# Half tiles of windowed attention: the globals' probabilities of four heads transposed as one 128x128 array instead of head by head

## The chip, the cores and the metric

The program runs on one core of a Trainium2 chip. The metric is the device time in microseconds of one execution. The kernel before has a median of 1014.69 us over 3 runs (1013.98 to 1016.17); one further execution was recorded by the profiler and took 1014.06 us.

## The reference

A windowed attention with global tokens feeds a two-layer network; the output is float32. There are 8 batches of 8 heads, 512 local tokens, 32 global tokens and 64 numbers per head. Local queries see the 32 globals and the local keys at most 32 positions away; global queries see everything.

```python
s_g  = scale * q_g @ concat(k_g, k_l).T          # 32 x 544 per head
s_l  = concat(scale * q_l @ k_g.T,               # 512 x 32: locals on globals
              where(|i - j| <= 32, scale * q_l @ k_l.T, -1e9))
out  = concat(softmax(s_g) @ v_all, softmax(s_l) @ v_all)   # v_all = concat(v_g, v_l)
x    = out as 4608 tokens x 512
h    = x @ w_in                                   # 512 x 2048
y    = elu(h) @ w_out                             # 2048 x 512
```

## The kernel before

Two streams of work share the engines. `attention()` (from L601) works in **tiles**: a tile is one batch, one group `g` of four heads, and 128 consecutive local queries `t` (0 to 3), so there are 8 x 2 x 4 = 64 tiles, 16 of them with t = 0. `ffn_stream()` (from L290) works through blocks of 256 tokens of the network: every float32 product there is three float16 matmuls of 256 columns (L306 for the first layer, L381 and L423 for the second). The program is written in turns of both streams (`pace`, L839), and a scheduler then fixes the order of each engine's queue, each served in order. While attention and network run, weights are loaded and converted to two float16 parts each (`unit`, L150 to L209), all of it early in the kernel.

A slot of attention is a tile or the global queries of a group (stage G, `stage_ga`, L625). The stages of a tile come in different slots:

- **S** (`stage_s`, L686): scores, 16 rows of L699; one array `p` holds, for each of the four heads, 128 columns of window keys and 32 columns of globals. VectorE masks and takes the maximum (L710), ScalarE exponentiates and sums (L717). Then `norm` (L720): VectorE forms 1/sum (L721, L722) and GpSimd scales the four heads' 160 columns (L724).
- **T** (`stage_t`, L730), two slots after S: four transposes of 128x128 turn the window part (L737); one copy puts them in `ptw` (L739).
- **U** (`stage_u`, L666), the same slot as T: the globals' part. For each head a matmul with the head's 32 columns as weights and the identity as the moving array puts 32 rows into PSUM (L673). In the tiles of t = 0 a 32x32 matmul for each head (L675) does the same with `pk`, the global queries' probabilities on the globals. One transpose (L676) turns `pg`, the global queries' probabilities on the tile's local keys. ScalarE copies to `ptw` (L677, L679) and `ptg` (L681; L684 for `pk`).
- **V** (`stage_v`, L742), one slot after T and U: 12 matmuls of `ptg` and `ptw` with the values (L766), and the copy to the network's input (L769).

A float32 matmul appears in the trace as two rows and a transpose as one, so U has 8 rows of L673, 8 of L675 where t = 0, and one of L676. The three `ptg` arrays are used alternately by the tiles of t > 0, the third by those of t = 0. In a loop of slots the stages are written in the order S, V, T, U (L823), loads two slots ahead (L799). All loads go through SyncE's queue; `qg`, the global queries, has two buffers (L616).

## Time and profile before

| | before |
|---|---|
| median of 3 runs | 1014.69 us |
| profiled execution | 1014.06 us |
| its span | 1012.3 us |
| TensorE busy | 979.0 us (97%) |
| VectorE busy | 737.2 us (73%) |
| ScalarE busy | 692.5 us (68%) |
| GpSimd busy | 248.1 us (25%) |

The span runs from the first to the last instruction; some 1.8 us of the execution's time lie around it. PE is TensorE's matmuls, PEld its weight loads (which run beside matmuls), DVE VectorE, ACT ScalarE, POOL GpSimd, SPq SyncE's DMA queue. Matmul rows are modelled to their end, so they overlap; what a step costs TensorE is read from start to start. In a row of the timeline, 128*32 is the part of the array in use (rows by columns), 128x128 the operand, x8 the number of merged rows.

### The profile page before, as it was taken

The page shows a single profiled execution, that of the slowest core. Times are in us where ns is not written, and L with a number is a line of the kernel's source. Part 1 is how long each engine was busy: PE and PEld are TensorE (multiplying, and loading weights), DVE is VectorE, ACT ScalarE, POOL GpSimd, SP SyncE. Part 2 cuts the span into 40 slices and gives each one's busy share as a digit, 9 for nine tenths or more (in the row PEclk, how much of TensorE's full clock was granted, in tenths as well). Part 3 has the DMA queues.
Part 4 walks back from the last instruction along what each step waited for, and adds up shares of the span by engine and source line. Part 5 has one row for each costly group of instructions (what it writes and reads, how often), then busy time and mean ns, then how long its engine had stood idle before and what let it go on. Part 6 is the DMA issues. An engine that isn't in the chain of part 4 may idle for free.

```text
span 1012.3 us, 24859 instructions
## 1 busy us (share of the span) xinstructions
PE 979.0 (97%) x9776; PEld 753.6 (74%) x9776; DVE 737.2 (73%) x2178; ACT 692.5 (68%) x1684; POOL 248.1 (25%) x435
## 2 busy tenths in 40 slices
PE   7799888999999999999999999999999999999997
PEld 3556555566666778877887888878878888888886
DVE  3757898999996667676776767676677758676665
ACT  4666968777666768676676667676776767677674
POOL 3534646626122111211212112111131121100000
PEclk9789998999999999999999999999999999999999
DMA  7645775653331123101420124112410111000000
GB/s 287 209 152 176 254 228 170 217 183 115 116 106 50 53 90 127 48 19 42 148 95 20 53 90 140 35 33 64 146 61 17 53 33 38 2 21 7 17 22 21
DMA packets 39372, 95.17 MB, mean 94 GB/s; under 512 B 5944, under 2 KB 6456, under 8 KB 39256
## 3 DMA queue, kind: packets, MB, share of 16 engines
q1 hardware_dynamic: 39064, 93.32, 27.2%
q8 instruction: 77, 1.26, 0.5%
q14 instruction: 39, 0.32, 0.1%
q10 hardware_dynamic: 144, 0.13, 0.0%
q0 software_dynamic: 48, 0.13, 0.0%
HBM read 78.36 MB, written 15.20 MB: 92 GB/s over the span
## 4 chain that ended last, share of the span: by engine, by line
PE 77%; DVE 8%; ACT 5%; issue 5%; POOL 2%; DMA 1%; POOLq 0%; ACTq 0%; DVEq 0%
PE h L306 27%; PE acc L423 12%; PE pa L766 6%; PE h L423 6%; PE acc L381 5%; PE pa L673 4%; PE pa L699 4%; PE pa L423 3%; PE pa L737 3%; PE pa L306 2%; PE pa L634 2%; PE pa L676 1%; POOL p L724 1%; PE h L766 1%; PE pa L675 1%
## 5 line engine op out<-in xcount | busy, mean ns | idle before, releaser
L306 PE MATMUL h<-xh,winh 128*128 128x256 f16 x992 | 271.5, 274 | 5.9 <-ACT hs L316 5.7
L306 PE MATMUL h<-xh,winl 128*128 128x256 f16 x992 | 270.7, 273 | 0.8 <-DVE winl L200 0.8
L306 PE MATMUL h<-xl,winh 128*128 128x256 f16 x992 | 270.8, 273 | 0.4 <-DVE xl L512 0.4
L306 PEld LDWEIGHTS <-winh 128*128 128x128 f16 x2176 | 209.5, 99 | 46.7 <-issue 15.5
L724 POOL TENSOR_SCALAR p<-p,sm 128x160 f32<-128x160 f32 x256 | 130.8, 528 | 433.9 <-DVE sm L722 198.2
L324 DVE SCALAR_TENSOR_TENSOR g<-g,hs 128x512 f32<-128x512 f32 x136 | 94.1, 692 | 125.8 <-ACT g L317 125.5
L423 PEld LDWEIGHTS <-gh 128*128 128x128 f16 x1456 | 140.4, 99 | 23.6 <-issue 6.1
L717 ACT ACTIVATE p<-p,m 128x160 f32<-128x160 f32 x256 | 106.4, 418 | 69.5 <-DVE m L713 68.9
L315 ACT ACTIVATE g<-h,xs 128x512 f32<-128x512 f32 x124 | 84.8, 684 | 53.0 <-PE h L306 51.9
L306 PEld LDWEIGHTS <-winl 128*128 128x128 f16 x1088 | 106.8, 98 | 15.5 <-DVE winl L200 1.4
L327 DVE SCALAR_TENSOR_TENSOR gl<-gs,xs,gh 128x640 f16<-128x640 f32 x104 | 93.0, 894 | 30.2 <-ACT gh L346 29.9
L346 ACT ACTIVATE gh<-gs,xs 128x640 f16<-128x640 f32 x104 | 86.3, 829 | 32.3 <-DVE gs L342 32.3
L345 ACT ACTIVATE gh<-g,xs 128x256 f16<-128x256 f32 x104 | 53.2, 512 | 56.0 <-DVE g L324 55.7
L423 PE MATMUL acc<-wouth,gh 128*128 128x256 f16 (+1 forms) x312 | 88.0, 282 | 0.2 <-ACT gh L346 0.2
L317 ACT ACTIVATE g<-g 128x512 f32<-128x512 f32 x136 | 85.5, 629 | 0.0
L423 PE MATMUL acc<-wouth,gl 128*128 128x256 f16 x312 | 85.0, 273 | 0.2 <-DVE gl L327 0.2
L316 ACT ACTIVATE hs<-h,xs 128x512 f32<-128x512 f32 x124 | 84.4, 681 | 1.0 <-POOL xs L526 1.0
L423 PE MATMUL acc<-woutl,gh 128*128 128x256 f16 x312 | 85.0, 273 | 0.0
L423 PEld LDWEIGHTS <-gl 128*128 128x128 f16 x728 | 71.2, 98 | 12.9 <-DVE gl L327 0.5
L327 DVE SCALAR_TENSOR_TENSOR gl<-g,xs,gh 128x256 f16<-128x256 f32 (+1 forms) x136 | 75.8, 558 | 6.9 <-ACT gh L331 3.4
L710 DVE CUSTOM_DVE_ANT_0 p<-pa,msk 128x160 f32<-128x160 f32 x228 | 62.2, 319 | 13.1 <-PE pa L699 13.0
L766 PE MATMUL pa<-ptw,v 128*64 128x96 f32 x864 | 54.0, 246 | 0.0
(217 smaller groups left out, 2037.1 us busy)
## 6 DMA issues: line engine op xcount, KB each, us to landing
v<-vT SPq DMA_DIRECT2D x64, 384.0 KB, 3.2
k<-kT SPq DMA_DIRECT2D x32, 640.0 KB, 5.1
q<-qT SPq DMA_DIRECT2D x32, 256.0 KB, 5.3
raw<-w_in SPq DMA_DIRECT2D x8, 1024.0 KB, 6.5
raw<-w_out SPq DMA_DIRECT2D x8, 1024.0 KB, 5.3
out<-o SPq DMA_DIRECT2D x32, 256.0 KB, 2.3
od<-o SPq DMA_DIRECT2D x24, 256.0 KB, 4.0
o<-od SPq DMA_DIRECT2D x24, 256.0 KB, 3.2
```

The source lines that it names most:

```text
L306: nc.tensor.matmul(h[:, j, :], wt[:, c, f], xt[:, c, :], start=k == 0, stop=k == 11)
L315: nc.scalar.activation(g, hf, AF.Relu, scale=sc[:, p:p + 1])
L316: nc.scalar.activation(hs, hf, AF.Copy, scale=sc[:, 2 * NP + 1 + p:2 * NP + 2 + p])
L317: nc.scalar.activation(g, g, AF.Exp, scale=-1.0)
L324: nc.vector.scalar_tensor_tensor(out=g, in0=g, scalar=-1.0, in1=hs, op0=ALU.add, op1=ALU.max)
L327: nc.vector.scalar_tensor_tensor(out=dst, in0=src, scalar=sg, in1=hi, op0=ALU.mult, op1=ALU.subtract)
L346: nc.scalar.activation(gh[:, 2:7, :], s, AF.Copy, scale=sg)
L423: nc.tensor.matmul(cols, gt, w, start=first, stop=last and k == len(todo) - 1)
L710: nc.vector.tensor_tensor_reduce(out=p, in0=sp[r][:, j * KW:(j + 1) * KW], in1=msk[:, mi, :], op0=ALU.add, op1=ALU.max, scale=1.0, scalar= ...
L717: nc.scalar.activation(ps[i], ps[i], AF.Exp, bias=m[:, 1, i:i + 1], scale=scale, accum_out=s[:, 0, i:i + 1])
L724: nc.gpsimd.tensor_scalar(ps[i], ps[i], s[:, 1, i:i + 1], 1.0, ALU.mult, ALU.mult)
L766: nc.tensor.matmul(pv[64 * r:64 * r + 64, o], w, x, start=i == 0, stop=i == 2)
```

## The change

The globals' part of `p` gets an array of its own, `pz` (128 queries x 4 heads x 32 globals), which VectorE writes normalized in one operation with 1/sum as a broadcast operand. GpSimd then scales only the 128 window columns. U turns `pz` with one transpose of 128x128. The exponentials of the global queries on the globals go into `pu`, and four GpSimd operations write them, normalized, into the diagonal blocks of a 128x128 array `pk` whose other entries are zero; U turns that with one transpose, and VectorE adds up its four column blocks into `ptg`. To make room in memory, there are two `ptg` instead of three (one for the tiles of t > 0, one for t = 0), and `qg` has one buffer.

```diff
-    ptg = [wts.tile([P, PW], F32, name=f"ptg{i}") for i in range(3)]
+    ptg = [wts.tile([P, PW], F32, name=f"ptg{i}") for i in range(2)]
...
+    pkd = [wts.tile([P, P], F32, name=f"pk{i}") for i in range(2)]
+    for p in (*ptg, *pkd):
         nc.gpsimd.memset(p, 0.0)
...
-            qg = apool.tile([P, 2, SG], F32, name="qg", bufs=2)
+            qg = apool.tile([P, 2, SG], F32, name="qg", bufs=1)
...
-            pk = apool.tile([P, 32], F32, name="pk")
+            pk = pkd[g]
+            pu = apool.tile([P, 32], F32, name="pu", bufs=1)
...
-                nc.gpsimd.tensor_scalar(pk, pk, s[:, 3:4], 1.0, ALU.mult, ALU.mult)
+                for h in range(4):
+                    q = slice(32 * h, 32 * h + 32)
+                    nc.gpsimd.tensor_scalar(pk[q, q], pu[q, :], s[q, 3:4], 1.0, ALU.mult, ALU.mult)
...
-            for h in range(4):
-                q = slice(32 * h, 32 * h + 32)
-                nc.tensor.matmul(tp[q, P:2 * P], st["p", g, t][:, h, P:KW], ident, start=True, stop=True)
-                if t == 0:
-                    nc.tensor.matmul(tp[q, 2 * P:2 * P + 32], pk[q, :], ident[q, q], start=True, stop=True)
+            nc.tensor.transpose(tp[:, P:2 * P], st["pz", g, t].rearrange("p h x -> p (h x)"), ident)
+            if t == 0:
+                nc.tensor.transpose(tp[:, 2 * P:3 * P], pk, ident)
...
-                nc.scalar.copy(pz[:, HQ:HQ + 32], tp[:, 2 * P:2 * P + 32])
+                nc.vector.tensor_reduce(out=pz[:, HQ:HQ + 32], in_=tp[:, 2 * P:3 * P].rearrange("p (h q) -> p q h", h=4),
+                                        op=ALU.add, axis=AX.X)
...
-                    nc.gpsimd.tensor_scalar(ps[i], ps[i], s[:, 1, i:i + 1], 1.0, ALU.mult, ALU.mult)
+                    nc.gpsimd.tensor_scalar(ps[i][:, 0:P], ps[i][:, 0:P], s[:, 1, i:i + 1], 1.0, ALU.mult, ALU.mult)
+                pz = st["pz", g, t] = apool.tile([P, 4, 32], F32, name="pz")
+                nc.vector.tensor_tensor(out=pz, in0=pp[:, :, P:KW], in1=s[:, 1, :].unsqueeze(2).to_broadcast([P, 4, 32]),
+                                        op=ALU.mult)
...
-            pt, pz = st["pt", g, t] = ptw[n % 2], ptg[2 if t == 0 else n % 2]
+            pt, pz = st["pt", g, t] = ptw[n % 2], ptg[t == 0]
```

Line numbers from the changed kernel are a few higher than those of before: L673 and L675 there become L675 (`pz`) and L677 (`pk`), L676 becomes L678, L737 L743, L766 L772, L699 L702, L423 L424.

Where both streams run densely, the queue of TensorE read like this before, at the U of a tile with t > 0 (`gh` and `gl` are the first layer's outputs in two parts, loaded as the array's weights; `raw` here holds sums of the second layer's weights, `h` a bank of PSUM):

```order
L423 LDWEIGHTS gl
L423 MATMUL h<-raw,gl 128x256
L673 MATMUL pa<-ident,p 32x128 x4
L676 MATMUL pa<-ident,pg 128x128
L423 LDWEIGHTS gh
L423 MATMUL pa<-raw,gh 128x256
```

and now, at the same tile:

```order
L424 LDWEIGHTS gl
L424 MATMUL h<-raw,gl 128x256
L675 MATMUL pa<-ident,pz 128x128
L678 MATMUL pa<-ident,pg 128x128
L424 LDWEIGHTS gh
L424 MATMUL pa<-raw,gh 128x256
```

Four matmuls became one transpose, and the neighbours stand where they stood. From the U of the 21st tile on (44 of the 64), TensorE's queue differs in the U stages alone.

At the start of the kernel TensorE's queue had this, the end of the U of the first tile, T and U of the second, and then the first V (`h<-ptg`, `h<-ptw`; the rows of L699 are the S of later tiles):

```order
L676 MATMUL pa<-ident,pg 128x128
L737 MATMUL pa<-ident,p 128x128 x4
L673 MATMUL pa<-ident,p 32x128 x4
L676 MATMUL pa<-ident,pg 128x128
L699 MATMUL acc<-k,q 64x160 x4
L699 MATMUL pa<-k,q 64x160
L699 MATMUL acc<-k,q 64x160 x4
L766 MATMUL h<-ptg_85,v 64x160 x2
L766 MATMUL h<-ptw_81,v 64x96 x4
```

and now has, from the U of the first tile:

```order
L675 MATMUL pa<-ident,pz 128x128
L677 MATMUL pa<-ident,pk_89 128x128
L678 MATMUL pa<-ident,pg 128x128
L743 MATMUL pa<-ident,p 128x128 x4
L772 MATMUL h<-ptg_84,v 64x160 x2
L772 MATMUL h<-ptw_81,v 64x96 x4
L772 MATMUL h<-ptg_84,v 64x160 x2
L772 MATMUL h<-ptw_81,v 64x96 x4
L702 MATMUL acc<-k,q 64x160 x4
L675 MATMUL pa<-ident,pz 128x128
L678 MATMUL pa<-ident,pg 128x128
```

The first V moved ahead of the second tile's U, and the order of the first 20 tiles, among the weights' conversion, was drawn up anew in such places.

On VectorE, in the dense part, the new operation stands right behind 1/sum (`sm`) and ahead of the low float16 parts `gl`, which the second layer's matmuls take:

```order
L343 TENSOR_TENSOR gs<-g 128x128
L724 TENSOR_SCALAR sm<-sm 128x4
L725 RECIPROCAL sm<-sm 128x4
L729 TENSOR_TENSOR pz<-p,sm 128x128
L328 SCALAR_TENSOR_TENSOR gl<-g,xs,gh 128x256
L328 SCALAR_TENSOR_TENSOR gl<-gs,xs,gh 128x640
```

There the rows of before read the same without L729.

More of the change, by code (lines that the diff above doesn't have):

```diff
@@ L108, in attn_ffn @@
         nc.gpsimd.memset(p[0:HQ, 1, :], 0.0)
-    for p in ptg:
+    pkd = [wts.tile([P, P], F32, name=f"pk{i}") for i in range(2)]
+    for p in (*ptg, *pkd):
         nc.gpsimd.memset(p, 0.0)
@@ L652, in ex @@
                                          AF.Exp, bias=m[:, 3:4], scale=scale, accum_out=s[:, i:i + 1])
-                nc.scalar.activation(pk, halves[0][:, NT * HQ:NT * HQ + 32], AF.Exp, bias=m[:, 3:4], scale=scale,
+                nc.scalar.activation(pu, halves[0][:, NT * HQ:NT * HQ + 32], AF.Exp, bias=m[:, 3:4], scale=scale,
                                      accum_out=s[:, 2:3])
```

## Prediction

> **What bounds the kernel now.** First the busy times in four stretches, then the chain of waits in the same stretches. Columns of the windows: length, then busy time and instructions of PE, PEld, DVE, ACT and POOL, then the granted TensorE clock, DMA share and GB/s.
>
> ```profile
> 0.00:95.00 95.00, 81.07 (x845) 50.28 (x846) 56.95 (x260) 54.91 (x201) 37.82 (x85) 0.86 0.58 202
> 95.00:235.00 140.00, 128.44 (x1084) 82.67 (x1083) 128.46 (x333) 109.31 (x237) 79.87 (x100) 0.98 0.65 217
> 235.00:870.00 635.00, 633.60 (x6611) 500.55 (x6609) 458.19 (x1379) 437.50 (x1099) 124.41 (x241) 1.00 0.20 68
> 870.00:1012.00 142.00, 135.86 (x1244) 120.06 (x1241) 93.62 (x211) 90.78 (x150) 5.95 (x10) 0.99 0.05 16
> ```
>
> From 235 us to 870 us TensorE is busy for 633.6 of 635 us, while VectorE and ScalarE have a quarter to a third of their time free. What leaves TensorE there leaves the kernel. Between 95 and 235 us the weights are converted: TensorE and VectorE are each busy for 128 of 140 us, and neither alone sets the end. In the head, up to 95 us, TensorE works for 81 us at a clock of 0.86. After 870 us no attention is left. The chain of waits says the same for the head and the dense stretch, in this order (shares of the stretch by line):
>
> ```profile
> by line: PE h L766 12.3%; PE pa L673 10.9%; PE pa L737 8.7%; PE pa L634 7.4%; PE pa L699 6.9%; PE h L306 5.4%; PE acc L133 4.7%; POOL p L724 4.1%; PE acc L699 3.5%; PE pa L676 3.5%; PE pa L675 3.3%; DVE p L710 2.9%; DVE cu L179 2.6%; issue
> ...
> by line: PE h L306 36.7%; PE acc L423 14.7%; PE pa L766 9.2%; PE h L423 7.3%; PE acc L381 6.7%; PE pa L699 4.3%; PE pa L673 4.0%; PE pa L423 3.6%; PE pa L737 2.9%; PE pa L676 1.8%; PE pa L634 1.4%; PE pa L675 1.1%; ACT hs L316 0.7%; ACT p L
> ```
>
> In the head the three lines of stage U (L673, L675, L676) make 17.7% of the chain, 16.8 us of 95: U is on the path there too.
>
> How many tiles lie where comes from the rows of L673 and L675 in the four stretches (PE busy and rows, PEld busy and rows):
>
> ```profile
> 0.00:95.00 95.00, 12.57 (x96) 4.07 (x96) 0.86 0.58 202
> 95.00:235.00 140.00, 5.80 (x64) 2.04 (x64) 0.98 0.65 217
> 235.00:870.00 635.00, 30.72 (x352) 10.84 (x352) 1.00 0.20 68
> ...
> 0.00:95.00 95.00, 4.30 (x32) 2.38 (x32) 0.86 0.58 202
> 95.00:235.00 140.00, 1.95 (x16) 1.06 (x16) 0.98 0.65 217
> 235.00:870.00 635.00, 9.74 (x80) 5.29 (x80) 1.00 0.20 68
> ```
>
> A tile has eight rows of L673, and with t = 0 also eight of L675. That makes 12 tiles in the head (4 with t = 0), 8 in the middle (2), and 44 in the dense stretch (10).
>
> **What a U costs, and what it will cost.** The timeline of TensorE shows a U of t > 0, a U of t = 0 and, for comparison, a stage T of four full transposes:
>
> ```profile
> 408.89 0.27 PE L423 MATMUL acc<-cu,gl 128*128 128x256 f16 x1
> 409.09 0.43 PE L673 MATMUL pa<-ident,p 128*32 128x128 f32 x8
> 409.45 0.33 PE L676 MATMUL pa<-ident,pg 128*128 128x128 f32 x1
> 409.62 0.27 PE L423 MATMUL h<-wouth,gh 128*128 128x256 f16 x1
> ...
> 326.51 0.27 PE L306 MATMUL h<-xh,winl 128*128 128x256 f16 x1
> 326.71 0.41 PE L673 MATMUL pa<-ident,p 128*32 128x128 f32 x2
> 327.05 0.24 PE L675 MATMUL pa<-ident,pk 32*32 32x32 f32 x2
> ...
> 328.75 0.33 PE L676 MATMUL pa<-ident,pg 128*128 128x128 f32 x1
> 328.92 0.27 PE L306 MATMUL h<-xh,winh 128*128 128x256 f16 x1
> ...
> 405.83 0.27 PE L306 MATMUL h<-xh,winl 128*128 128x256 f16 x1
> 405.94 0.60 PE L737 MATMUL pa<-ident,p 128*128 128x128 f32 x4
> 406.38 0.27 PE L306 MATMUL h<-xh,winh 128*128 128x256 f16 x1
> ```
>
> A float16 matmul occupies TensorE for 0.11 us (405.83 to 405.94). So the U of t > 0 takes from 408.89 + 0.11 = 409.00 to 409.62, 0.62 us, and the U of t = 0 from 326.62 to 328.92, 2.30 us: there the pieces alternate between 32 columns of all rows and 32x32 corners, and each pair takes 0.5 us. The four transposes of T take 0.44 us, 0.11 each, with no gap on either side. After the change U consists of such transposes alone, two or (t = 0) three: 0.22 or 0.33 us. The saving is 0.40 us for t > 0 and 1.97 us for t = 0. The other bound is L676's own 0.17 us for each transpose (409.45 to 409.62), behind narrow matmuls: 0.28 and 1.79 us. I take T's, since the new transposes stand among full-array work.
>
> - **Dense stretch:** 10 x 1.97 + 34 x 0.40 = 33.3 us (by the other bound 10 x 1.79 + 34 x 0.28 = 27.4). TensorE's order there changes in nothing else. I take 33.
> - **Head:** 4 x 1.97 + 8 x 0.40 = 11.1 us at full clock, 12.9 at 0.86. From it go the three debits below; I take 7.
> - **Middle:** 2 x 1.97 + 6 x 0.40 = 6.3 us of TensorE work, but other engines end last there, and VectorE gets 8 `pz` and 2 reductions more; I take 2, with bounds of 6 either way because the order is drawn anew.
>
> **The other terms.** The nearest rows for the new VectorE operations, and for what GpSimd and ScalarE change (in the rows with three numbers, durations are ns minimum/median/maximum):
>
> ```profile
> L342 DVE TENSOR_TENSOR gs<-g x104: 270/284/703, 333.1 to 1001.9; 128x128 f32<-128x128 f32 x104
> L121 DVE TENSOR_REDUCE xm<-pa 128x1 f32<-128x128 f32 x16 | 4.5, 282 | 3.3 <-PE pa L120 3.1
> L684 ACT COPY ptg<-pa 128x32 f32<-128x32 f32 x16 | 3.1, 192 | 0.0
> L724 POOL TENSOR_SCALAR p<-p,sm x256: 387/398/1879, 13.9 to 846.5; 128x160 f32<-128x160 f32 x128
> L660 POOL TENSOR_SCALAR pk<-pk,sg x16: 285/656/970, 12.6 to 776.3; 128x32 f32<-128x32 f32 x16
> PEld pa L737 <- POOL p L724: 10.5, 15, 4.3
> ```
>
> VectorE gains 64 x 0.28 us + 16 x 0.28 = 22 us (64 `pz` at up to 0.70 make 45), ScalarE loses 16 x 0.19 = 3 us. In the dense stretch 44 + 10 of these are 15 us on an engine with 177 us free; there `gl` comes 0.28 us later, which the weights loaded two steps behind cover. Without that cover it would cost 44 x 0.28 = 12 us. In the middle the cover is thin: 10 x 0.28 = 2.8 us, already inside my 2.
>
> GpSimd scales 128 instead of 160 columns, which is below 0.40 us an operation, and writes `pk` in four pieces instead of one: 3 x 0.29 = 0.9 us more per group at best, 3 x 0.97 = 2.9 at worst, ahead of `pg` and of `p` in its queue. With GpSimd at a fifth of the dense stretch this is hidden. In the head T waits for `p` (10.5 us over the whole head and 15 times, in the last row), and four groups there cost between nothing and 4 x 2.9 = 12 us; I take 1, since a group's `pk` and `pg` are usually done before the next `sm` comes.
>
> `pz` is written in the same moment as GpSimd scales the same tile. L724's spread, 398 at the median and 1879 at the most, and L342's 703 beside its 284 say that both can stretch when they meet. I charge the head 2 us (12 tiles of some 0.2), bounded by 0 and 12 x 0.42 = 5. On this the Trainium skill (GPSIMD Engine Reference, Specifications) says that GpSimd's memory interfaces are shared with VectorE, with contention for VectorE instructions that read two arrays from SBUF, as the new one does and the old GpSimd-only way did not. The rows above agree in that durations spread.
>
> The single `qg` buffer makes the second `qg` load wait for the first G to end, with the keys of the second group and the first weights behind it in SyncE's queue:
>
> ```profile
> 4.75 0.49 SPq L617 DMA_DIRECT2D qg<-qgT  x1
> 7.44 0.39 PE L634 MATMUL pa<-k,qg 64*32 64x256 f32 x2
> 12.86 0.41 PE L634 MATMUL pa<-k,qg 64*32 64x256 f32 x2 [3.35 <-ACT p L717]
> k<-kT SPq DMA_DIRECT2D x32, 640.0 KB, 5.1
> ```
>
> The load moves from 4.75 to 7.44 + 0.39 = 7.8 us, 3.1 us later. The two key loads behind it then land near 7.8 + 0.5 + 1.9 (their two issues) + 5.1 = 15.3 us; the second G starts at 12.86 now. So the cost lies between 0 and 3 us; I take 2. Debits of the head: 1 + 2 + 2, and 1 for idle time that stays: 12.9 - 6 = 7.
>
> One `ptg` for all tiles of t > 0: ScalarE's copy of U (L681) must now wait for V of the tile before, and behind it in ScalarE's queue stand the network's exponentials. V comes first in TensorE's queue anyway; it costs nothing as long as that gap stays (the last rival).
>
> **Sum:** 33 + 7 + 2 = 42 us; 1014 - 42 = **972 us** against the profiled execution's 1014.06, which lies 0.6 us under the median. A difference of 0.2%, 2 us, is about what a measurement of this kernel tells from none.
>
> **The rivals.**
>
> 1. *Only the dense stretch gains (chance 0.18).* The head's savings are taken by `p` and the keys arriving later, and the new order of the middle gives back up to 6. For it: 14 us of the head without TensorE work, and VectorE as full as TensorE in the middle. Against it: U's 17.7% of the head's chain. Time: 1014 - 33 = 981, up to 1014 - 33 + 6 = 987.
> 2. *Everything counts (0.08).* The head's 12.9 and the middle's 6 come in full: 1014 - 33 - 13 - 6 = 962. For it: TensorE is busy for 128 of 140 us in the middle. Against it: the debits.
> 3. *The clock falls (0.03).* Transposes replace matmuls in the head, and if these did not keep the clock up, the head's 81 busy us at 0.86 would run at the 0.7 of the second slice: 81 x 0.86 / 0.7 = 99.5, 18 us longer. Time: 1014 - 33 - 2 + 18 = 997, still faster.
>
> ```profile
> PEclk9789998999999999999999999999999999999999
> ```
>
>    Against it: T, L676 and every other transpose run now at a granted clock of 1.00. The rule behind it is the Trainium skill's (TensorE: Matmul & The Clock Gate, Part 4: PE-mode transpose): transposes do not count as busy for the clock. In the dense stretch a U's 0.2 us is too short to show it, so the row for 235 to 870 us neither proves nor excludes it.
> 4. *The single `ptg` stalls ScalarE (0.02), the one that ends slower.* Place: L681 behind V.
>
> ```profile
> 403.86 0.50 PE L766 MATMUL pa<-ptw,v 128*64 128x96 f32 x8
> ```
>
>    V of the tile before ends at 404.36, U starts at 409.09: 4.7 us to spare. If V came behind U's copy instead, ScalarE would hold the network's work for each tile. To turn 42 us into a loss TensorE would have to stand still for 42 / 64 = 0.66 us a tile; at 1 us a tile the time is 1014 - 42 + 64 = 1036.
>
> That TensorE's work would not get shorter at all is no case of its own: the U rows and T's rows lie a factor of two to seven apart, and L676's 0.17 us is the worst that a transpose costs.
>
> **Chances.** The forecast has 0.67, with a range of its own from 964 to 980 (the bounds of the head's debits, 7 with 1 to 13, and of the middle in part). Half of rival 1 up to 986 and most of rival 2 belong to the range: 961 to 986. Rivals 1 to 3 and the forecast all end faster; slower has rival 4's 0.02 and 0.01 for what is not foreseen, and 0.01 stays for no change, which makes 0.96, 0.01 and 0.03.
>
> **What would show it.** In the profile after: U of t > 0 from start to start 0.22 us and U of t = 0 0.33 us, with no gap ahead; the dense stretch (from the 21st tile's U on) shorter by 33 us, with TensorE still at 99%; L729 near 0.28 us and VectorE's busy time up by some 22 us; the second G starting 2 us later. Wrong would be: waits of PE for ACT or DVE in the dense stretch of over 5 us, transposes at 0.17 us, a lower clock in the head, or a middle that is longer than 140 us.

## The result, and the profile after

The changed kernel takes 973.72 us (median of 4 runs, 973.07 to 977.49) against 1015.43 us for the kernel before (4 runs, 1013.98 to 1016.25): a ratio of 0.9598, with an interval of 0.9571 to 0.9626. Its profiled execution took 974.17 us, with a span of 972.1 us; before it was 1014.06 and 1012.3. Forecast were 972 us, in a range of 961 to 986. Three executions on record stand far off all others (1112.72 and 3332.99 us of the kernel before, 1116.83 us of the one with one `qg` buffer); the ratios leave them out, and without them the medians given here change by less than 0.1 us.

First the four stretches in the windows of the changed kernel, cut at the places in its work that are nearest to those shown of before (columns as there):

```profile
0.00:89.00 89.00, 69.31 (x781) 46.92 (x781) 64.71 (x288) 59.11 (x207) 47.35 (x103) 0.90 0.67 233
89.00:225.00 136.00, 119.21 (x975) 78.00 (x974) 124.35 (x331) 104.79 (x225) 72.70 (x103) 0.97 0.64 216
225.00:830.00 605.00, 601.84 (x6224) 492.89 (x6223) 467.44 (x1431) 434.02 (x1088) 135.85 (x270) 1.00 0.21 71
830.00:972.00 142.00, 135.69 (x1242) 119.89 (x1240) 93.81 (x211) 90.90 (x150) 5.96 (x10) 0.99 0.05 16
```

TensorE is still busy for 99% of the dense stretch, which is 30 us shorter. The clock did not fall: 0.90 in the head, where it was 0.86, 0.97 in the middle, where it was 0.98, and 1.00 in the dense stretch. GpSimd now works for 47 us in a head of 89 us. The stretch without attention is as long as before.

The timeline of TensorE shows a U of t > 0 and a U of t = 0:

```profile
402.55 0.27 PE L307 MATMUL h<-xh,winl 128*128 128x256 f16 x1
402.66 0.27 PE L675 MATMUL pa<-ident,pz 128*128 128x128 f32 x1
402.77 0.27 PE L678 MATMUL pa<-ident,pg 128*128 128x128 f32 x1
402.88 0.27 PE L307 MATMUL h<-xh,winh 128*128 128x256 f16 x1
...
423.11 0.27 PE L307 MATMUL h<-xh,winl 128*128 128x256 f16 x1
423.22 0.27 PE L675 MATMUL pa<-ident,pz 128*128 128x128 f32 x1
423.33 0.27 PE L677 MATMUL pa<-ident,pk 128*128 128x128 f32 x1
423.44 0.27 PE L678 MATMUL pa<-ident,pg 128*128 128x128 f32 x1
423.55 0.27 PE L424 MATMUL acc<-wouth,gh 128*128 128x256 f16 x1
```

From start to start that is 0.22 and 0.33 us, 0.11 for each transpose, without a gap on either side. U took 0.62 and 2.30 us before.

For an account by place the same U is looked up in both traces. These are the U of the 21st and of the 64th tile, in the kernel before:

```profile
269.96 0.43 PE L673 MATMUL pa<-ident,p 128*32 128x128 f32 x8
...
868.90 0.42 PE L673 MATMUL pa<-ident,p 128*32 128x128 f32 x8
```

and in the changed kernel:

```profile
259.94 0.27 PE L675 MATMUL pa<-ident,pz 128*128 128x128 f32 x1
...
829.03 0.27 PE L675 MATMUL pa<-ident,pz 128*128 128x128 f32 x1
```

The 21st U comes 10.0 us earlier. From there to the 64th it was 598.94 us and is 569.09, 29.85 us less. Behind the 64th the last 143.4 us became 143.1, one U's worth. That makes 40.2 us, the difference of the spans.

The new and changed operations, each grouped over the whole span (ns minimum/median/maximum):

```profile
L729 DVE TENSOR_TENSOR pz<-p,sm x64: 274/291/419, 13.6 to 810.1; 128x128 f32<-128x128 f32 x64
L686 DVE TENSOR_REDUCE ptg<-pa x16: 276/282/292, 19.8 to 777.5; 128x32 f32<-128x128 f32 x16
L664 POOL TENSOR_SCALAR pk<-pu,sg x64: 282/294/2257, 12.5 to 743.9; 32x32 f32<-32x32 f32 x64
L727 POOL TENSOR_SCALAR p<-p,sm x256: 368/375/2046, 14.8 to 808.1; 128x128 f32<-128x128 f32 x128
```

VectorE's operations cost what the nearest rows had said, 0.29 and 0.28 us. GpSimd's pieces of `pk` are 0.29 us at the median, but up to 2.26. VectorE's busy time rose from 737.2 to 750.3 us, by 13 us and not by the 22 of the forecast, though the two new groups make 64 x 0.291 + 16 x 0.282 = 23 us; neighbouring rows overlap in the trace, and how much of the difference that explains stays open.

The second `qg` load in the timeline of SyncE's queue, and the second G in that of TensorE:

```profile
8.02 0.33 SPq L618 DMA_DIRECT2D qg<-qgT  x1
```

```profile
14.60 1.07 PE L635 MATMUL pa<-k,qg 64*32 64x256 f32 x4 [5.19 <-DMA k<-kT]
```

The load moved from 4.75 to 8.02 us, and the second G from 12.86 to 14.60.

TensorE's waits in the dense stretch, before (the stretch from 235 to 870 us) and after (225 to 830 us); the numbers are us in total, times, the longest:

```profile
PE h L306 <- ACT hs L316: 1.1, 3, 0.5
```

```profile
PE h L307 <- ACT hs L317: 2.8, 6, 0.9
```

It is one wait in both kernels: the first layer's matmuls need a bank of PSUM that ScalarE still reads for `hs`. It became longer. In the chain of waits ScalarE and VectorE now have a larger place in this stretch, where the first of them was `hs` with 0.7% before (shares by line):

```profile
by line: PE h L307 27.5%; PE acc L424 11.2%; PE pa L772 7.2%; PE h L424 5.6%; DVE gl L328 3.7%; PE acc L382 3.5%; ACT p L720 3.3%; PE pa L702 3.2%; DVE g L325 2.8%; PE pa L424 2.7%; DVE p L713 2.4%; issue 2.2%; PE pa L743 2.2%; DVE cu L260 
```

The longest of these waits, from the timeline of the changed kernel (start, duration, engine; in brackets the idle time ahead and what ended it):

```profile
761.50 0.32 DVE L713 CUSTOM_DVE_ANT_0 p<-pa,msk 128x160 f32<-128x160 f32 x1
762.54 0.16 DVE L716 TENSOR_SCALAR m<-m 128x4 f32<-128x4 f32 x1
762.79 0.43 ACT L720 ACTIVATE p<-p,m 128x160 f32<-128x160 f32 x1 [1.48 <-DVE m L716]
...
764.71 0.68 ACT L316 ACTIVATE g<-h,xs 128x512 f32<-128x512 f32 x1
...
764.84 0.27 PE L424 MATMUL pa<-raw,gl 128*128 128x256 f16 x1
...
765.29 0.68 ACT L317 ACTIVATE hs<-h,xs 128x512 f32<-128x512 f32 x1
...
766.01 0.27 PE L307 MATMUL h<-xh,winh 128*128 128x256 f16 x1 [0.90 <-ACT hs L317]
```

Read upwards: TensorE stands from 764.95 to 766.01 us for `hs`; `hs` stands in ScalarE's queue behind four exponentials of S (L720); and the first of those waited 1.48 us for the maxima, which VectorE had in its own queue. Counted from start to start, matmuls that came more than 0.35 us after the one ahead were 4 between the 21st and the 64th U before, and 8 after, all of them of the first layer. Beyond a matmul's 0.11 us they cost 1.9 us before and 4.4 us after. Below these are called the stalls.

### The profile page after: what moved, and what is told of

It reads as the page before. It is cut to its first block, busy times and chain, and to the rows that moved or that the text cites. A ratio compares the mean times of both kernels' runs of the same rounds, so it can differ in the third digit from the quotient of the medians.

```text
span 972.1 us, 23882 instructions
## 1 busy us (share of the span) xinstructions
PE 926.0 (95%) x9216; PEld 737.7 (76%) x9216; DVE 750.3 (77%) x2258; ACT 688.8 (71%) x1668; POOL 261.9 (27%) x484
## 4 chain that ended last, share of the span: by engine, by line
PE 60%; DVE 18%; ACT 10%; issue 7%; DMA 4%; POOL 1%; SPq 0%; POOLq 0%; DVEq 0%; ACTq 0%
PE h L307 21%; PE acc L424 10%; PE pa L772 5%; PE h L424 5%; PE acc L382 4%; PE pa L702 3%; ACT p L720 3%; DVE gl L328 3%; PE pa L307 2%; PE pa L424 2%; PE pa L743 2%; DVE g L325 2%; DVE p L713 2%; PE pa L635 2%; DVE cu L260 1%
## 5 line engine op out<-in xcount | busy, mean ns | idle before, releaser
L307 PEld LDWEIGHTS <-winh 128*128 128x128 f16 x2176 | 208.8, 98 | 47.0 <-issue 16.1
L727 POOL TENSOR_SCALAR p<-p,sm 128x128 f32<-128x128 f32 x256 | 124.7, 505 | 374.7 <-DVE sm L725 142.3
L424 PEld LDWEIGHTS <-gh 128*128 128x128 f16 x1456 | 139.2, 98 | 23.6 <-issue 6.1
L720 ACT ACTIVATE p<-p,m 128x160 f32<-128x160 f32 x256 | 106.3, 418 | 60.6 <-DVE m L716 59.8
L307 PEld LDWEIGHTS <-winl 128*128 128x128 f16 x1088 | 106.8, 98 | 14.4 <-DVE winl L201 1.0
L424 PE MATMUL acc<-wouth,gh 128*128 128x256 f16 (+1 forms) x312 | 88.0, 282 | 0.2 <-ACT gh L347 0.2
L424 PE MATMUL acc<-wouth,gl 128*128 128x256 f16 x312 | 85.1, 273 | 0.2 <-DVE gl L328 0.2
L424 PE MATMUL acc<-woutl,gh 128*128 128x256 f16 x312 | 85.0, 273 | 0.0
L424 PEld LDWEIGHTS <-gl 128*128 128x128 f16 x728 | 71.2, 98 | 12.9 <-DVE gl L328 0.5
L664 POOL TENSOR_SCALAR pk<-pu,sg 32x32 f32<-32x32 f32 x64 | 41.0, 640 | 66.4 <-ACT gh L347 24.5
```

The source lines that it names most:

```text
L307: nc.tensor.matmul(h[:, j, :], wt[:, c, f], xt[:, c, :], start=k == 0, stop=k == 11)
L424: nc.tensor.matmul(cols, gt, w, start=first, stop=last and k == len(todo) - 1)
L720: nc.scalar.activation(ps[i], ps[i], AF.Exp, bias=m[:, 1, i:i + 1], scale=scale, accum_out=s[:, 0, i:i + 1])
L727: nc.gpsimd.tensor_scalar(ps[i][:, 0:P], ps[i][:, 0:P], s[:, 1, i:i + 1], 1.0, ALU.mult, ALU.mult)
```

## The experiments

The first question was why U had been so dear. The theory, at which the prediction only hints ("the pieces alternate"): the change of the array's shape between 128x32 and 32x32 costs the time, not the number of rows. The rivals: the sixteen small matmuls themselves cost it, so that only leaving them out helps; or the gain comes from what VectorE takes off GpSimd. The second question was where the dense stretch lost 3 us, and what the head really paid. Numbers of all runs stand in a table at the end of this section.

**The kernel before, with the matmuls of U sorted by shape.** No work is removed.

```diff
             for h in range(4):
                 q = slice(32 * h, 32 * h + 32)
                 nc.tensor.matmul(tp[q, P:2 * P], st["p", g, t][:, h, P:KW], ident, start=True, stop=True)
-                if t == 0:
-                    nc.tensor.matmul(tp[q, 2 * P:2 * P + 32], pk[q, :], ident[q, q], start=True, stop=True)
+            for h in range(4 if t == 0 else 0):
+                q = slice(32 * h, 32 * h + 32)
+                nc.tensor.matmul(tp[q, 2 * P:2 * P + 32], pk[q, :], ident[q, q], start=True, stop=True)
```

> The kernel before, with one edit: in the U of t = 0 the four 32x32 matmuls of pk stand behind the four matmuls of p instead of between them. No work is removed. Theory 1 (a U of t = 0 took 2.30 us because TensorE changes eight times between 32 columns of all rows and 32x32 corners, at some 0.2 us a change, and the matmuls themselves are cheap): the U of t = 0 falls to about 0.9 us, 1.4 us x 16 = 22 us less TensorE work, of which 14 lie in the dense stretch and most of the other 8 in the head; time 995 to 998. Theory 2 (each of the 16 rows costs its 0.1 us wherever it stands): the U stays above 2 us, time within 3 us of before.

Measured: 992.24 us, ratio 0.9779 (0.9756 to 0.9802). The U of t = 0 in its timeline of TensorE:

```profile
318.41 0.43 PE L673 MATMUL pa<-ident,p 128*32 128x128 f32 x8
318.76 0.26 PE L676 MATMUL pa<-ident,pk 32*32 32x32 f32 x8
318.96 0.33 PE L677 MATMUL pa<-ident,pg 128*128 128x128 f32 x1
319.12 0.27 PE L306 MATMUL h<-xh,winh 128*128 128x256 f16 x1
```

The same seventeen rows take 0.71 us (318.41 to 319.12) instead of 2.2, and the dense stretch is 14.4 us shorter (584.55 us). That the rows cost their time wherever they stand is refuted: sorting alone gives 22.7 of the change's 41 us by the medians. The total came out 3 us below the range that was expected. On this the Trainium skill (TensorEngine Tiling (Array Packing), Key Properties) says that changing the tiling mode drains the TensorE; the trace agrees in that seven changes between the two shapes became one, and 1.5 us went, 0.25 for each of the six. The rows also show what a change spoils. One 128x32 matmul by itself lasts 0.41 us (the row at 326.71 of the kernel before, x2), and four side by side last 0.43 (409.09, x8); with 32x32 it is 0.24 (327.05, x2) and 0.26 (318.76, x8). Four of a shape that stand together run nearly as one, and a matmul of the other shape between them prevents it. How much of the 0.25 us is the change itself and how much this lost overlap, no run here separates.

**The change without the block-diagonal array**: `pz` with one transpose, `pk` as before but its four matmuls together.

```diff
-            pk = pkd[g]
+            pk = apool.tile([P, 32], F32, name="pk")
...
-                for h in range(4):
-                    q = slice(32 * h, 32 * h + 32)
-                    nc.gpsimd.tensor_scalar(pk[q, q], pu[q, :], s[q, 3:4], 1.0, ALU.mult, ALU.mult)
+                nc.gpsimd.tensor_scalar(pk, pk, s[:, 3:4], 1.0, ALU.mult, ALU.mult)
...
-                nc.tensor.transpose(tp[:, 2 * P:3 * P], pk, ident)
+                for h in range(4):
+                    q = slice(32 * h, 32 * h + 32)
+                    nc.tensor.matmul(tp[q, 2 * P:2 * P + 32], pk[q, :], ident[q, q], start=True, stop=True)
...
-                nc.vector.tensor_reduce(out=pz[:, HQ:HQ + 32], in_=tp[:, 2 * P:3 * P].rearrange("p (h q) -> p q h", h=4),
-                                        op=ALU.add, axis=AX.X)
+                nc.scalar.copy(pz[:, HQ:HQ + 32], tp[:, 2 * P:2 * P + 32])
...
```

> The changed kernel without the block-diagonal pk: pk is normalized and transposed as before, by four 32x32 matmuls, but these now stand together behind the transpose of pz. Theory 1 (changes of the array's mode are what costs): the U of t > 0 takes 0.22 us and that of t = 0 about 0.7 us, so TensorE saves 48 x 0.40 + 16 x 1.6 = 45 of the 50.6 us; time about 978. Theory 2 (the pk matmuls themselves cost): the U of t = 0 stays near 1.9 us, the saving is 48 x 0.40 + 16 x 0.4 = 26 us, time about 992.

Measured: 972.51 us, 0.9594 (0.957 to 0.9618), not to be told from the whole change, and 5 us below the expected 978. Its U of t = 0:

```profile
309.65 0.27 PE L671 MATMUL pa<-ident,pz 128*128 128x128 f32 x1
309.85 0.26 PE L675 MATMUL pa<-ident,pk 32*32 32x32 f32 x8
310.04 0.33 PE L676 MATMUL pa<-ident,pg 128*128 128x128 f32 x1
310.21 0.27 PE L306 MATMUL h<-xh,winh 128*128 128x256 f16 x1
```

0.56 us against the change's 0.33: over the dense stretch's ten that is 2.3 us, of which 0.8 come back as shorter stalls (570.58 against 569.09 us in all). Before the 21st U this kernel is 5.6 us ahead, but its profiled execution had a clock of 0.97 up to there, against 0.95, which makes some 5 us. So the block-diagonal array, its four pieces on GpSimd and its sum on VectorE bring nothing over a sorted order that these runs can show.

**The change without `pz`**: the globals by four matmuls, GpSimd scaling all 160 columns, `pk` block-diagonal.

```diff
-            nc.tensor.transpose(tp[:, P:2 * P], st["pz", g, t].rearrange("p h x -> p (h x)"), ident)
+            for h in range(4):
+                q = slice(32 * h, 32 * h + 32)
+                nc.tensor.matmul(tp[q, P:2 * P], st["p", g, t][:, h, P:KW], ident, start=True, stop=True)
...
```

> The changed kernel without pz: GpSimd scales all 160 columns again, and U turns p by four matmuls of 32 columns, then pk by one transpose of 128x128. By the sum over start-to-start times: U of t > 0 stays at 0.62 us, that of t = 0 falls from 2.30 to about 0.73 us, 16 x 1.57 = 25 us of TensorE work; 16 of it in the dense stretch, so 994 to 998. If instead the gain of the change came from VectorE's pz (an earlier, cheaper GpSimd scaling) and not from TensorE's rows, this kernel would stay within 5 us of before.

Measured: 989.31 us, 0.9758 (0.9733 to 0.9783). U takes 0.62 us for t > 0 as before, and 0.72 with `pk`'s transpose; 583.42 us lie between the 21st and the 64th U. More than half of the gain is there although VectorE and GpSimd work on `p` as they did before. That this gain comes from what VectorE takes off GpSimd is refuted. The dense stretch is 15.5 us shorter, as expected (16); the total lies 5 us below the expected range, and what is more lies ahead of the 21st U, where this execution's clock was 0.97 instead of 0.94.

**The change with two `qg` buffers** (and two `m` and `sm` instead of three, to make room).

```diff
-            qg = apool.tile([P, 2, SG], F32, name="qg", bufs=1)
+            qg = apool.tile([P, 2, SG], F32, name="qg", bufs=2)
...
-            m = apool.tile([P, 2, 4], F32, name="m", bufs=3)
-            s = apool.tile([P, 2, 4], F32, name="sm", bufs=3)
+            m = apool.tile([P, 2, 4], F32, name="m", bufs=2)
+            s = apool.tile([P, 2, 4], F32, name="sm", bufs=2)
```

> The changed kernel with two buffers for qg again (the space comes from two instead of three buffers for m and sm). Theory 1 (the second qg load waits for the first G, and the keys of the second group with it): the second qg load is issued near 4.8 instead of 8.0 us, the second G starts near 12.9 instead of 14.6 us, and the head is 1.5 to 2 us shorter: 971.5 to 972.5. Theory 2 (GpSimd's scaling decides when the first T's start, whatever the second G does): the second G starts earlier and the time stays within 0.7 us of the changed kernel's 973.7.

Measured: 974.30 us, 0.9603 (0.9578 to 0.9628). The second G starts at 12.61 us instead of 14.60, and the time stays. The late load is real and costs nothing that these runs can show. The buffers also changed the order of TensorE's queue at some places between 36 and 52 us, so this is not the load alone.

**ScalarE relieved**: U's copy of the globals on VectorE in the dense part (there `tab` holds an "f").

```diff
-            nc.scalar.copy(pz.rearrange("p (a x) -> p a x", a=2)[:, :, 0:HQ],
-                           tp[:, P:2 * P].rearrange("p (a q) -> p a q", a=2))
+            copy = nc.vector.tensor_copy if "f" in tab else nc.scalar.copy
+            copy(pz.rearrange("p (a x) -> p a x", a=2)[:, :, 0:HQ],
+                 tp[:, P:2 * P].rearrange("p (a q) -> p a q", a=2))
```

> The changed kernel with U's copy to ptg moved from ScalarE to VectorE where both streams run densely (44 or so copies of 0.27 us); TensorE's order is the same. It asks why the dense stretch became 30 us shorter and not 33: in the changed kernel TensorE waits there 2.8 us, six times, for hs of the network's first layer (ScalarE). Theory 1 (ScalarE is late because VectorE is: before hs, ScalarE's queue stands idle for the scores' maxima m): VectorE gets fuller, the six waits stay or grow, from the U of tile 21 to that of tile 64 it takes 569 us or more; time 973.5 to 977. Theory 2 (ScalarE has too much work): the waits fall below 1 us, this stretch takes 566.5 us, time 971.

Measured: 977.98 us, 0.9651 (0.9618 to 0.9684). The waits of TensorE between 270 and 840 us:

```profile
PE h L307 <- ACT hs L317: 2.7, 7, 0.6
PE pa L773 <- DVE ptg L684: 2.0, 2, 1.1
```

The wait for `hs` stays, and V now waits for `ptg` on VectorE. Of this kernel's 14 stalls 8 are of the first layer, 4.1 us, as many as in the change (4.4 us). It isn't the amount of ScalarE's work that stalls TensorE.

**`pz` written twice**, the same operation two times in a row.

```diff
                 nc.vector.tensor_tensor(out=pz, in0=pp[:, :, P:KW], in1=s[:, 1, :].unsqueeze(2).to_broadcast([P, 4, 32]),
                                         op=ALU.mult)
+                nc.vector.tensor_tensor(out=pz, in0=pp[:, :, P:KW], in1=s[:, 1, :].unsqueeze(2).to_broadcast([P, 4, 32]),
+                                        op=ALU.mult)
```

> The changed kernel with the VectorE operation that writes pz done twice for each tile (64 x 0.28 = 18 us more on VectorE, 12 of them between the U of tile 21 and that of tile 64); the output is the same. Theory 1 (VectorE's added work is hidden up to the waits for hs, which come from VectorE): the dense stretch goes from 569 to 570 to 573 us, the part before it gets up to 3 us longer, time 974 to 979. Theory 2 (wholly hidden): 973.7 within 1 us. Theory 3 (VectorE is on the path everywhere): 12 us in the dense stretch alone, time 986 or more.

Measured: 978.53 us, 0.9638 (0.9598 to 0.9677). Between the 21st and the 64th U lie 568.82 us, as without the second copy; the 4.8 us by the medians can only lie outside that stretch. That was a miss: an effect in the dense stretch had been expected too. The 4.8 us are no price of the operation: the ratio's interval overlaps the change's (0.9571 to 0.9626), the runs go from 973.92 to 981.25 us, and TensorE's order was drawn anew from 39 us on.

**`pz` by GpSimd in the dense part**, four operations a tile.

```diff
+                if "f" in tab:
+                    for i in range(4):
+                        nc.gpsimd.tensor_scalar(pz[:, i, :], pp[:, i, P:KW], s[:, 1, i:i + 1], 1.0, ALU.mult, ALU.mult)
+                else:
+                    nc.vector.tensor_tensor(out=pz, in0=pp[:, :, P:KW],
+                                            in1=s[:, 1, :].unsqueeze(2).to_broadcast([P, 4, 32]), op=ALU.mult)
```

> The changed kernel with pz written by GpSimd (four operations of 32 columns) instead of VectorE where both streams run densely; TensorE's order there is the same. Theory 1 (the 3 us missing in the dense stretch are VectorE's added 0.28 us a tile): the waits for hs fall to the 1.1 us of before, from the U of tile 21 to that of tile 64 it takes 567 us instead of 569, time 971.5 to 972.5. Theory 2 (they come from TensorE reaching the network's matmuls earlier, whatever VectorE does): waits and stretch stay, 569 us, time 973.7.

Measured: 974.08 us, 0.9603 (0.9583 to 0.9622); 568.92 us and 8 stalls, as in the change. VectorE's `pz` doesn't cause the stalls. In the change VectorE stands idle until U releases `pz` (3.5 us, 5 times by the trace); here, in the dense stretch, that wait is gone with the operation, and the time is the same.

**The pieces of `pk` written twice** on GpSimd, with TensorE's order as it is.

```diff
                     nc.gpsimd.tensor_scalar(pk[q, q], pu[q, :], s[q, 3:4], 1.0, ALU.mult, ALU.mult)
+                    nc.gpsimd.tensor_scalar(pk[q, q], pu[q, :], s[q, 3:4], 1.0, ALU.mult, ALU.mult)
```

> The changed kernel with each of GpSimd's four pieces of pk written twice (4 x 0.64 us more in each of the 16 groups on GpSimd, 41 us in all); TensorE's order is the same. Theory 1 (the pieces stand ahead of pg and p in GpSimd's queue and cost time where T waits for p, up to the weights' conversion): the U of tile 21 starts 3 to 8 us later than in the changed kernel's 259.9, the dense stretch stays at 569, time 977 to 982. Theory 2 (done before the next sm comes, as the prediction took it for all but 1 us): within 1.5 us of 973.7.

Measured: 980.24 us, 0.9673 (0.9626 to 0.9719), 6.5 us over the change by the medians, with intervals that just touch at 0.9626 and runs from 976.89 to 986.29 us; 569.09 us between the 21st and the 64th U, unchanged. Four more pieces a group are hidden in the dense stretch and dear before it. The clock may have a share in that: its median is 0.981 against 0.986, 0.005 x 972 = 4.9 us of full clock, and whether the longer waits lowered it or chance did stays open.

**The exponentials and the norm of S one step later** in the dense part, so that they stand behind `hs` in ScalarE's queue and wait less for the maxima.

```diff
+            late = 1 if "f" in tab else 0
             for i in range(4):
-                defer(2 + i // 2, lambda i=i: ex(i))
-            defer(4, norm)
+                defer(2 + late + i // 2, lambda i=i: ex(i))
+            defer(4 + late, norm)
```

> The changed kernel with the exponentials of S (and the normalization behind them) written one step later where both streams run densely; in ScalarE's queue one or two of a tile's four exponentials then stand behind the network's g and hs instead of ahead. TensorE's order is the same. Theory 1 (the six waits of TensorE for hs come from hs standing behind exponentials that wait for the scores' maxima): the waits fall from 2.8 us to below 1.2, from the U of tile 21 to that of tile 64 it takes 567 us instead of 569.1, time 971 to 972. Theory 2 (hs is late for another reason): 569 us and 973.7. If T then waits for p, the stretch gets longer instead.

Measured: 972.44 us, 0.9592 (0.9564 to 0.9619), within the interval of the change. The dense stretch shows the effect, in the waits of TensorE between 270 and 840 us and in the two U:

```profile
PE h L307 <- ACT hs L317: 1.9, 3, 1.0
```

```profile
259.50 0.27 PE L675 MATMUL pa<-ident,pz 128*128 128x128 f32 x1
...
827.01 0.27 PE L675 MATMUL pa<-ident,pz 128*128 128x128 f32 x1
```

567.51 us instead of 569.09; of the 8 stalls 5 are left, 3.0 us instead of 4.4. So the place in ScalarE's queue is the cause of 1.4 us of the stalls, about half of what the change added. The longest stall, the one shown above, is not among those that went:

```profile
764.05 0.27 PE L307 MATMUL h<-xh,winh 128*128 128x256 f16 x1 [0.96 <-ACT hs L317]
```

There all four exponentials still stand ahead of `hs`, and the first still waits 1.48 us for the maxima, so this edit left that place nearly as it was.

**The kernel before with one `qg` buffer**, and **the kernel before with two `ptg`**, each alone.

```diff
-            qg = apool.tile([P, 2, SG], F32, name="qg", bufs=2)
+            qg = apool.tile([P, 2, SG], F32, name="qg", bufs=1)
```

> The kernel before with one buffer for qg, nothing else. By the prediction's debit for it: the second qg load waits for the first G, the second G starts some 2 us later than the 12.86 of before, and the time rises by 0 to 3 us, to 1014.5 to 1017.5. Rival: hidden, because GpSimd's scaling of p ends last there anyway; the second G later, the U of tile 21 unchanged at 270, the time within 0.7 us of before.

```diff
-    ptg = [wts.tile([P, PW], F32, name=f"ptg{i}") for i in range(3)]
+    ptg = [wts.tile([P, PW], F32, name=f"ptg{i}") for i in range(2)]
...
-            pt, pz = st["pt", g, t] = ptw[n % 2], ptg[2 if t == 0 else n % 2]
+            pt, pz = st["pt", g, t] = ptw[n % 2], ptg[t == 0]
```

> The kernel before with two ptg instead of three (one for all tiles of t > 0), nothing else. By the prediction it costs nothing where both streams run densely, since V stands ahead of the next U in TensorE's queue with some 4.7 us to spare: 599 us from the U of tile 21 to that of tile 64, ScalarE's copy not waiting for V. At the start V is moved ahead of the second U. Time within 1.5 us of before. Rival (the copy stalls ScalarE): the stretch grows by 0.3 us a tile or more, 13 us, time above 1025.

Measured: with one `qg` 1011.73 us, 0.9977 (0.996 to 0.9993), the second G 1.2 us later (14.10 us) and the time no longer; with two `ptg` 1009.32 us, 0.9956 (0.9941 to 0.9971). Both are misses, since neither was expected to gain. The two U with two `ptg`:

```profile
265.00 0.43 PE L673 MATMUL pa<-ident,p 128*32 128x128 f32 x8
...
863.96 0.43 PE L673 MATMUL pa<-ident,p 128*32 128x128 f32 x8
```

598.96 us between them, as in the kernel before (598.94). All of the 5 us lies ahead of the 21st U. What was expected of the start did not happen; the first V still stands behind the second U, which starts at 22.66 us:

```profile
25.43 0.80 PE L766 MATMUL h<-ptg,v 128*64 128x160 f32 x4
```

In both controls the fewer buffers make the scheduler lay out TensorE's order anew later in the head, from some 47 us on with one `qg` and from some 50 us on with two `ptg`. ScalarE did not wait for V behind the 21st U, and ahead of it once, 1.2 us.

**The parts that help, together**: `pz` with a sorted `pk`, two `qg` buffers, and the later exponentials.

> The kernel with pz alone (pk by four small matmuls standing together, no pieces on GpSimd), with two buffers for qg and the later exponentials. By theory 1 of the others: U of t = 0 at 0.56 us, the U of tile 21 near 253 us (254.3 with pz alone, less what the second qg buffer brings), from there to the U of tile 64 568 us (570.6 less the waits for hs), time 967 to 971. If the second qg buffer and the later exponentials bring nothing, 972.5 as with pz alone.

Measured: 969.46 us (5 runs, 968.79 to 972.19), 0.9566 (0.9539 to 0.9594). By the medians that is 4.3 us below the change; the intervals overlap. The distance to the 64th U is 569.24 us, above the expected 568.

All runs, with medians in us; from the profiled execution the start of the 21st U, the clock granted up to there, the distance from it to the 64th, and the stalls in between (number, us beyond 0.11 each; with the copy on VectorE 6 of them, with two `qg` one, are not of the first layer); and the median of the granted clock over the runs (for the kernel before over 35 that ran beside the others):

| kernel | median | 21st U | clock up to it | to the 64th | stalls | clock |
|---|---|---|---|---|---|---|
| before | 1015.43 | 269.96 | 0.94 | 598.94 | 4, 1.9 | 0.982 |
| change | 973.72 | 259.94 | 0.95 | 569.09 | 8, 4.4 | 0.986 |
| before, sorted by shape | 992.24 | 261.65 | 0.95 | 584.55 | 5, 2.4 | 0.986 |
| change, `pk` sorted | 972.51 | 254.31 | 0.97 | 570.58 | 6, 3.6 | 0.986 |
| change without `pz` | 989.31 | 259.92 | 0.97 | 583.42 | 4, 1.9 | 0.989 |
| change, two `qg` | 974.30 | 256.94 | 0.95 | 569.65 | 9, 5.1 | 0.984 |
| change, copy on VectorE | 977.98 | 260.94 | 0.94 | 572.36 | 14, 7.8 | 0.985 |
| change, `pz` twice | 978.53 | 266.43 | 0.94 | 568.82 | 9, 4.4 | 0.984 |
| change, `pz` on GpSimd | 974.08 | 257.90 | 0.96 | 568.92 | 8, 4.5 | 0.985 |
| change, pieces twice | 980.24 | 271.25 | 0.92 | 569.09 | 8, 4.4 | 0.981 |
| change, exponentials later | 972.44 | 259.50 | 0.95 | 567.51 | 5, 3.0 | 0.983 |
| before, one `qg` | 1011.73 | 265.01 | 0.95 | 598.96 | 4, 1.9 | 0.984 |
| before, two `ptg` | 1009.32 | 265.00 | 0.94 | 598.96 | 4, 1.9 | 0.985 |
| the best parts | 969.46 | 256.16 | 0.94 | 569.24 | 3, 2.3 | 0.985 |

The distance to the 64th U repeats to a tenth of a us wherever the order is the same (598.94, 598.96, 598.96). The 21st U doesn't repeat like that: it goes with the clock up to it, of which 0.01 makes 2.6 us, and a single profiled execution fixes it to some 5 us only.

## Why the prediction was right

- **What a U costs: exact.** T's row was the right one to take, with 0.11 us for each transpose and no gap. L676's 0.17 us, the other bound, belongs to a transpose that stands behind narrow matmuls, as the sorted kernels show (318.96 to 319.12).
- **Dense stretch, 33 us: 29.85 measured.** By the U's alone it should have been 33 x 0.40 + 10 x 1.97 = 32.9 between the two marks (of the 44 tiles the last U lies outside). The missing 3.0 us are the step that failed, "TensorE's order there changes in nothing else": the order didn't change, but its neighbours' pace didn't either. TensorE arrives earlier at the first layer's matmuls and stands for `hs`. The stalls make 2.5 of the 3.0 (4.4 - 1.9). Another 0.35 us is in S, from start to start 29.32 us instead of 28.97. That `pz` isn't the cause is shown by the two kernels that doubled it or moved it; that the queue of ScalarE is, by the later exponentials, for 1.4 of the 2.5 us. What causes the other 1.1 us stays open; the longest stall alone makes 1.06 of the change's 4.4 us, and the later exponentials left it.
- **Head and middle, 7 + 2 = 9 us: 10.0 measured, but from other terms.** The pieces of `pk` were charged 1 us: written twice, they make the kernel 6.5 us longer by the medians. `pz` was charged 2 us in the head and stood within the middle's 2; the 4.8 us of the kernel that writes it twice are not clear of noise and of a new order, so its price stays open; its rows take 0.42 us at most, where the prediction had feared 0.70. In the head the pieces of `pk` stand like this, in the timeline of GpSimd:

```profile
12.52 1.51 POOL L664 TENSOR_SCALAR pk<-pu,sg 32x32 f32<-32x32 f32 x4 [8.63 <-DVE m L716]
...
23.01 3.91 POOL L664 TENSOR_SCALAR pk<-pu,sg 32x32 f32<-32x32 f32 x4
```

  The second four take 3.9 us, 3.2 more than the 0.66 of the one piece that they replace; the prediction had 2.9 more as its worst for a group. All that GpSimd has queued waits behind them. A second copy need not cost what the first one does, and the clock may have a share, so the 6.5 us are a sign of the size and no exact price. One cost stands nowhere in the sum: V now waits for the sum of `pk`'s blocks on VectorE, where ScalarE made a copy before. In the middle, with the weights' conversion ahead of it in VectorE's queue, TensorE stood still for it:

```profile
195.82 0.53 PE L772 MATMUL pa<-ptg,v 128*64 128x160 f32 x2 [2.79 <-DVE ptg L686]
```

  A wait of 1.9 to 4.1 us for this sum on TensorE is in every trace that has both it and `pz`, and in neither of the two with a sorted `pk`, which do without the sum. The load of `qg` was charged 2 us: the second G did come 1.7 us later (14.60 against 12.86), but neither kernel that changed the buffers of `qg` shows a cost (both with an order drawn anew in places). Part of what made up for the debits can be the clock, which the sum held at that of before: by the windows, 95 x 0.14 + 140 x 0.02 = 16.1 us of full clock were lost before the dense stretch, and now 89 x 0.10 + 136 x 0.03 = 13.0, at most 3 us less. What else made up for them stays open; the new order is the nearest candidate, since the buffers alone moved the kernel before by 3 to 5 us. That the total is so close is partly luck.
- **One `ptg`, 0 us:** right for the dense stretch, which is unchanged with two `ptg` alone and in which ScalarE waits for no V. In the head it does, where it never did in the kernel before (ScalarE's wait, whole span; us in total, times, the longest):

```profile
ACT ptg L683 <- PE h L772: 1.2, 2, 0.9
```

  What was not foreseen is that the buffer count alone redraws the head, and that the kernel before gets 5 us faster by it, some of that with the clock (last section).
- **The rivals.** Only the dense stretch gains: no, 10 us came ahead of it. Everything counts: no, 29.85 of 33 and 10 of 19. The clock falls: no, it rose. The rule of the Trainium skill that stood behind this (TensorE: Matmul & The Clock Gate, Part 4: PE-mode transpose, transposes not counting as busy) is not seen in the head's mean clock, 0.90 after 0.86, though a head with more transposes and fewer matmuls is where it should show; the single steps in the last section don't settle it. The single `ptg` stalls: not in the dense stretch, 1.2 us in the head.

## What to carry to other kernels

Before small matmuls are removed, sort them by the part of the array that they use: here the order alone was worth more than half of the change, and the rest could be had with less new work. Where TensorE is busy for 99%, count its time from start to start; the sum then holds within a tenth, and what is missing is found at the next queue that TensorE runs into. Compare heads over several runs and a control that changes only the buffers, because a redrawn order and the clock move them by as much as a small edit.

## What the runs showed of the hardware

Each change between the 128x32 and the 32x32 part of the array that was sorted away brought 0.25 us, in which the lost overlap of neighbours is included (four 128x32 matmuls side by side last 0.43 us, one 0.41). A 128x32 matmul behind full-array work starts 0.09 us late (269.96 in the kernel before instead of 269.87), as a 32x32 one does (309.85 with `pk` sorted, instead of 309.76). A float32 transpose of 128x128 among full-array float16 matmuls costs 0.11 us, as much as such a matmul.

The clock falls to 0.50 in steps of 3.4 us. Here, in two windows of the changed kernel, one follows a stretch in which TensorE was busy for 8.2 of 13.6 us:

```profile
110.00:123.60 13.60, 8.16 (x61) 5.37 (x63) 12.00 (x19) 10.68 (x16) 4.84 (x9) 1.00 0.42 138
123.60:127.00 3.40, 3.40 (x16) 1.32 (x13) 3.40 (x9) 1.10 (x2) 0.00 (x0) 0.50 0.82 314
```

Idle time isn't the only cause. Two neighbouring windows of the kernel before:

```profile
44.10:68.00 23.90, 23.37 (x314) 15.41 (x310) 16.05 (x82) 17.50 (x74) 8.95 (x23) 1.00 0.64 209
68.00:78.20 10.20, 9.39 (x65) 5.52 (x67) 2.85 (x19) 4.76 (x17) 3.40 (x10) 0.50 0.06 14
```

TensorE was busy for 23.4 of 23.9 us, and then ran three such steps at half the clock. The last 3.4 us ahead of the drop look different, and so does an earlier window of the same kernel:

```profile
64.60:68.00 3.40, 2.88 (x20) 1.28 (x15) 1.86 (x9) 2.92 (x14) 1.52 (x4) 1.00 0.31 110
16.80:20.20 3.40, 3.11 (x24) 1.75 (x23) 1.22 (x5) 0.64 (x3) 0.20 (x1) 1.00 1.04 401
```

In the first TensorE was busy for 2.88 us, and apart from the end of an S it ran T's transposes and U's small matmuls alone. The second holds nothing but transposes and U's small matmuls, 3.11 us of them, and the clock stayed at 1.00 behind it. The Trainium skill (TensorE: Matmul & The Clock Gate, Part 1: The HAM clock gate) has a free-running window of 3.4 us and half the clock after an idle one; the length of the steps agrees. The drop at 68 us has no idle window ahead of it, so this doesn't give it, and what sets it stays open, the share of transposes and small matmuls among the candidates. Runs of one kernel differ with the clock: the change took 973.1 to 974.2 us at clocks of 0.985 to 0.987 and 977.5 us at 0.980. Part of the gain of the two controls can be of this kind as well, with 0.984 and 0.985 where the kernel before has 0.982: 0.002 x 1012 = 2 us and 0.003 x 1012 = 3 us of full clock, against 2.7 and 5.1 us of their medians (1014.41 us for the kernel before, beside those two).
